# Every second attention head of the last two chunks: scores with tokens on the partitions, one wide transposing DMA, and value products with the values stationary

## The chip, the cores and the metric

The kernel runs on one core of one Trainium2 chip. The metric is the device time of the whole program in microseconds (us). One execution was also recorded by the hardware profiler; the rows of its page and of its trace are what the text argues from. TensorE (PE in the profile) does the matrix products, ScalarE (ACT) the exponentials, VectorE (DVE) copies and elementwise work, GpSimd (POOL) a few tiny operations, and SyncE (SP) issues most DMAs. A "turn" below is a DMA that transposes blocks of 128 x 128 elements on the way.

## The reference

The program is a transformer block with adaptive layer norm on 2048 tokens of width 1024: `x + ga * attention(layernorm(x) * (1 + ca) + sa)`, then the same with a gated feed-forward layer, where the six vectors come from `silu(c) @ w_mod`. The part that the change touches is the attention:

```
q = (x @ wq).reshape(B, Sq, 32, 128)           # 32 query heads of 128
k, v = the last 512 cached keys and values, 4 heads, each repeated for 8 query heads
scores = einsum('bhqd,bhkd->bhqk', q, k) * 128 ** -0.5
p = softmax(scores, axis=-1)
o = einsum('bhqk,bhkd->bhqd', p, v)
return o.transpose(0, 2, 1, 3).reshape(B, Sq, 4096) @ wo
```

## The kernel before

The tokens are worked in 4 chunks of 512. Attention runs in one loop over `i`, where head number `i` goes from 0 to 127 (chunk `i // 32`, head `i % 32`). An iteration of the loop emits, in this order on TensorE: the query projection of head `i + 3` (`qproj`, 8 products 512 columns wide), the scores of head `i - 1` (`scores`, 4 products 512 wide, into the PSUM banks 0 to 3), and the value products of head `i - 2` (`pv`). After the last head of a chunk, `oproj` multiplies the finished heads with `wo` (256 products 512 wide); this place is called the seam. In the last three iterations pieces of the last chunk's `oproj` take the place of `qproj`. The feed-forward layer follows.

In `scores` the keys are stationary, so the exponentials come out with keys on the partitions and tokens along the row: two ACT instructions on 1024 elements a row (L813). `pv` then holds a 128 x 128 block of exponentials stationary and moves the values, with a column of ones beside them, so each product is 129 columns wide and a head takes 16 of them. The 129th column is the sum of the softmax: DVE takes its reciprocal (L831) and multiplies it in (L834), and a turn of 128 x 512 (L837) brings the result from tokens on the partitions to head columns on the partitions, into `oT_all`, which `oproj` reads.

Every operation is emitted through one tracker, which adds semaphore waits for what an operation reads and overwrites. Each engine works through its own instructions in the order of emission, and so does SP's queue of DMAs. An operation of DVE or ACT that overwrites a buffer which the same engine wrote before waits for that engine's own earlier operation.

Other work is spread over the iterations by tables. `LOADT` gives the iterations at which one of 24 columns of `w_mod` is loaded by a turn (`load_mt`, L588); four iterations later `mod_col` multiplies it with `silu(c)` and sums on DVE (L593). `load_wq` (L357) fetches the projection weights of four heads, 1 MB, every fourth iteration. `ln_task` is a generator for the layer norm of a later chunk: statistics, normalisation, a turn of 128 x 1024 (L454), later the scaling; `run_bg(1)` takes one step of it at the end of each iteration. `resid` is the end of an `oproj` product on DVE and uses two tiles `tmp`.

## Time and profile before

| what | us |
|---|---|
| median of 3 runs (lowest, highest) | 1270.17 (1270.08, 1270.31) |
| time of the profiled execution | 1270.14 |
| its span in the profile | 1268.3 |
| TensorE busy | 1255.1 (99%) |
| VectorE busy | 485.1 (38%) |
| ScalarE busy | 341.6 (27%) |

TensorE is busy throughout, at full clock (PEclk 9 in all 40 slices). The other engines' busy shares are means over very different stages: DVE and ACT are busiest in the attention loops, which fill about the first half of the span, and DMA is uneven there. The last two chunks' attention lies between about 362 us, where the second chunk's `oproj` ends, and 640 us; the third chunk's `oproj` stands between them.

### The profile page before, as it was taken

What the parts mean: (1) busy time and instruction counts of PE and PEld (TensorE: products, weight loads), DVE (VectorE), ACT (ScalarE), POOL (GpSimd) and SP (SyncE); (2) the same over time, 40 slices, a digit from 0 to 9 for tenths busy, and PEclk for the clock granted to TensorE, in tenths of its full rate; (3) what the DMA queues carried; (4) which work ended last, traced back from release to release, by engine and by line L of the source; (5) the groups of instructions that cost most, each with busy time, mean ns of one, the idle gap of its engine ahead of it and who ended that gap; (6) DMA issues with size and microseconds to landing.
All of it is one profiled execution on the core that took longest, in us unless ns stands there. A gap on an engine that the chain in (4) does not pass through costs nothing.

```text
span 1268.3 us, 17609 instructions
## 1 busy us (share of the span) xinstructions
PE 1255.1 (99%) x7442; PEld 640.7 (51%) x7583; DVE 485.1 (38%) x894; ACT 341.6 (27%) x389; POOL 56.0 (4%) x95
## 2 busy tenths in 40 slices
PE   8999999999999999999999999999999999999999
PEld 5655545555455554555544444444444444444444
DVE  4676226764257641365322321233212321222122
ACT  4655205553035550155510111011100111011100
POOL 1530000000000000000000000000000000000000
PEclk9999999999999999999999999999999999999999
DMA  9998306875029641064243972055512644034200
GB/s 320 264 263 218 92 1 127 177 171 125 1 57 177 138 114 34 9 129 123 61 145 100 291 246 94 25 158 150 168 40 72 177 141 134 17 128 154 67 9 25
DMA packets 239997, 156.67 MB, mean 124 GB/s; under 512 B 133296, under 2 KB 225840, under 8 KB 239920
## 3 DMA queue, kind: packets, MB, share of 16 engines
q1 hardware_dynamic: 181664, 96.83, 31.6%
q10 hardware_dynamic: 58256, 58.73, 14.6%
q8 instruction: 59, 0.97, 0.3%
q14 instruction: 18, 0.15, 0.1%
HBM read 119.93 MB, written 4.20 MB: 98 GB/s over the span
## 4 chain that ended last, share of the span: by engine, by line
PE 98%; issue 1%; DMA 0%; SPq 0%; DVE 0%
PE ps L271 98%; DMA arena<-in_w_mod_dram 0%; SPq L309 0%; SPq L334 0%; PE ps L275 0%; DVE arena L496 0%; DVE tmp L853 0%; DVE arena L855 0%; DVE gain_f L486 0%
## 5 line engine op out<-in xcount | busy, mean ns | idle before, releaser
L271 PE MATMUL ps<-arena 128*128 128x512 bf16 (+1 forms) x7213 | 1249.3, 333 | 10.1 <-POOL arena L298 2.0
L271 PEld LDWEIGHTS ps<-arena 128*128 128x128 bf16 x7354 | 632.9, 98 | 621.5 <-issue 2.1
L813 ACT ACTIVATE arena<-ps 128x1024 bf16<-128x1024 f32 x256 | 261.9, 1023 | 345.1 <-PE ps L271 333.4
L1059 ACT ACTIVATE arena<-ps 128x512 bf16<-128x512 f32 x112 | 66.9, 597 | 499.6 <-PE ps L271 499.6
L1060 DVE TENSOR_TENSOR arena<-ps,arena 128x512 bf16<-128x512 f32 x112 | 77.5, 692 | 276.2 <-PE ps L271 276.2
L853 DVE TENSOR_TENSOR tmp<-ps,rowb 128x512 f32<-128x512 f32 (+1 forms) x65 | 44.4, 683 | 318.8 <-PE ps L271 318.8
L644 DVE CAST arena<-ps 128x512 bf16<-128x512 f32 x120 | 82.8, 690 | 47.7 <-PE ps L271 47.7
L834 DVE TENSOR_TENSOR arena<-ps,rl 128x512 bf16<-128x512 f32 x128 | 88.5, 691 | 4.7 <-DVE rl L831 0.2
L831 DVE RECIPROCAL rl<-ps 128x4 f32<-128x4 f32 x128 | 23.4, 182 | 114.1 <-PE ps L271 114.1
L429 POOL TENSOR_SCALAR rstd<-mv 128x1 f32<-128x1 f32 x28 | 6.1, 216 | 910.3 <-DVE mv L428 910.3
L424 DVE BATCH_NORM_STATS2 st<-x_res 128x6 f32<-128x512 bf16 x62 | 42.4, 683 | 3.4 <-DMA x_res<-in_A_x_dram 3.3
L593 DVE SCALAR_TENSOR_TENSOR arena<-arena 128x1024 bf16<-128x1024 bf16 x24 | 29.2, 1215 | 0.0
L855 DVE TENSOR_TENSOR arena<-tmp,x_res 128x512 bf16<-128x512 f32 (+2 forms) x33 | 22.3, 677 | 1.1
L855 DVE TENSOR_TENSOR x_res<-tmp,x_res 128x512 bf16<-128x512 f32 x32 | 22.2, 693 | 1.1
L440 DVE TENSOR_SCALAR arena<-arena,gain,mod_bf 128x512 bf16<-128x512 bf16 x56 | 21.2, 420 | 0.0
L435 DVE TENSOR_SCALAR nsc<-x_res,mv,rstd 128x1024 bf16<-128x1024 bf16 x30 | 19.2, 641 | 0.0
L431 POOL TENSOR_TENSOR rstd<-rstd,mhalf 128x1 f32<-128x1 f32 x28 | 15.7, 559 | 2.3
L772 POOL TENSOR_SCALAR arena<-arena,sc_bf 128x512 f32<-128x512 bf16 x8 | 12.9, 1614 | 0.5 <-POOL arena L774 0.2
L774 POOL TENSOR_TENSOR arena<-arena 128x512 f32<-128x512 f32 x8 | 10.1, 1265 | 0.7
L428 DVE BATCH_NORM_AGGREGATE mv<-st 128x2 f32<-128x12 f32 x28 | 5.8, 209 | 1.0
L271 PEld LDWEIGHTS ps<-sc_bf,arena 128*128 128x128 bf16 x128 | 4.4, 96 | 1.4 <-DMA arena<-in_w_mod_dram 0.3
L271 PE MATMUL ps<-sc_bf,arena 128*128 128x1 bf16 x128 | 4.7, 164 | 0.3 <-DMA arena<-in_w_mod_dram 0.3
(56 smaller groups left out, 59.4 us busy)
## 6 DMA issues: line engine op xcount, KB each, us to landing
arena<-in_A_wq_dram SPq DMA_DIRECT2D x30, 1024.0 KB, 5.8
arena<-in_B_w_gate_dram ACTq DMA_DIRECT2D x28, 1024.0 KB, 5.4
arena<-in_B_w_up_dram ACTq DMA_DIRECT2D x28, 1024.0 KB, 7.9
arena<-in_A_wo_dram SPq DMA_DIRECT2D x8, 1024.0 KB, 7.6
arena<-in_B_w_down_dram SPq DMA_DIRECT2D x7, 1024.0 KB, 8.3
out_dram<-arena SPq DMA_DIRECT2D x15, 256.0 KB, 2.0
x_res<-in_A_x_dram SPq DMA_DIRECT2D x3, 1024.0 KB, 7.0
arena<-arena SPq DMA_TRANSPOSE x132, 2.6
```

What stands on the lines that cost most here:

```text
L271: T.op(PE, lambda: TE.matmul(out_ap, lhsT, rhs, start=start, stop=stop, skip_group_check=skip), reads=reads, writes=[bank_buf])
L424: T.op(DVE, lambda: V.bn_stats(st_[sl][:, hf * 6:hf * 6 + 6], x_res[:, t, hf * 512:hf * 512 + 512]), reads=[B_x[t]], writes=[B_st[sl]])
L440: T.op(DVE, lambda: V.tensor_scalar(dst[:, dt, :], dst[:, dt, :], gain[gi][:, dt:dt + 1], mod_bf[:, ccol + dt:ccol + dt + 1], op0=ALU.mult ...
L593: T.op(DVE, lambda: V.scalar_tensor_tensor(mt[n % 2], mt[n % 2], 1.0, sc_row, op0=ALU.mult, op1=ALU.mult, accum_out=mcol[:, n:n + 1]), rea ...
L644: T.op(DVE, lambda: V.tensor_copy(qT_s[qs], bank(b)), writes=[PB[b], B_qT[qs]])
L813: T.op(ACT, lambda: A.activation(ex_s[es][:, 2 * kp:2 * kp + 2, :], banks2(SCB + 2 * kp), AF.Exp, scale=att_scale), writes=[PB[SCB + 2 * k ...
L831: T.op(DVE, lambda: V.reciprocal(rl[r][:, :].rearrange("p (a b) -> p a b", a=2), psap(PVB * 512 + P, [[512, 2], [130, 2]])), writes=both + ...
L834: T.op(DVE, lambda: V.tensor_tensor(o_s[os_].rearrange("p (a b) d -> p a b d", a=2), psap(PVB * 512, [[512, 2], [130, 2], [1, P]]), rlb, A ...
L853: T.op(DVE, lambda: V.tensor_tensor(tmp[s][:, 0:n], bank(b, n), rowb[ri][:, c0:c0 + n], ALU.mult), reads=[B_row[ri]], writes=[PB[b], B_tmp ...
L855: T.op(DVE, lambda: V.tensor_tensor(dst[:, c0:c0 + n], tmp[s][:, 0:n], x_res[:, t, c0:c0 + n], ALU.add), reads=[B_tmp[s], B_x[t]], writes= ...
L1059: T.op(ACT, lambda: A.activation(sg_s[ss], bank(gb), AF.Silu), writes=[PB[gb], B_sg[ss]])
L1060: T.op(DVE, lambda: V.tensor_tensor(guT[:, ft, :], bank(ub), sg_s[ss], ALU.mult), reads=[B_sg[ss]], writes=[PB[ub], B_gu[ft]])
```

## The change

Heads 66, 68, ..., 126 (31 heads, the set `NAT`) go another way. Heads 64 and all odd heads keep theirs.

- `nat_scores`: the queries of 128 tokens are stationary and all 512 keys move, 4 products 512 wide. The exponentials have tokens on the partitions; they are four ACT instructions on 512 elements a row, and each also gives the sum of its row (`accum_out`). They are emitted one iteration earlier than `scores` would be, in the odd iteration before, in the place that the missing `scores` leaves.
- `nat_norm`: DVE takes the reciprocals of the sums and multiplies them in, in two halves: a reciprocal of 128 x 2 and two in-place `tensor_scalar` of 128 x 512 each, from bf16 to bf16 in SBUF. The first half follows `pv` in the odd iteration, the second follows `qproj` in the even one.
- `nat_turn`: one turn of 128 x 2048 (512 KB) brings keys onto the partitions.
- `nat_pv`: the values are stationary, the turned exponentials move: 4 products 512 wide into one bank. The result already stands in the layout of `oT_all`, and one DVE copy out of PSUM puts it there. The turn of 128 x 512 (L837), the reciprocal of 128 x 4 and the multiplication of 128 x 512 are gone for these heads. `nat_pv` comes two iterations after the head's turn is issued.
- At a seam (iterations 65 and 97) `nat_scores` and both halves of `nat_norm` come after `pv` and before `oproj`, and the turn after `oproj`.
- The buffers: the exponentials of these heads alternate between the first of the two `ex` tiles and the two `tmp` tiles, which become one tensor. The turned ones lie in two slots of 4 KB whose place moves twice (`PTAT`).
- `load_wq` is emitted before the scores, not behind `pv`, from iteration 65 on. The loads of `w_mod` columns go to every second iteration (33, 35, ..., 79) where they were 9 iterations to 4; what follows the last of them comes 6 iterations earlier. `run_bg` is called in other iterations, twice in some.

The diff, cut to its core:

```diff
+            NAT0 = 2 * Hq + 2
+            NAT = set(range(NAT0, NA, 2))
+            B_pn = [[_Buf("pn0_%d" % hf) for hf in range(2)], B_tmp]
+            pn = [None, tmp_t[:, :].bitcast(BF16)]
...
+            def nat_scores(i):
...
+                for j in range(TPC):
+                    mm(bank(SCB + j), qT_s[qs][:, j * P:(j + 1) * P],
+                       kT_sb[:, gk * KT:(gk + 1) * KT, :].rearrange("p a b -> p (a b)"), True, True,
+                       [B_kT[gk], B_qT[qs]], PB[SCB + j])
+                for j in range(TPC):
+                    T.op(ACT, lambda: A.activation(pn[s][:, j * 512:(j + 1) * 512], bank(SCB + j), AF.Exp, scale=att_scale,
+                                                   accum_out=psum[s][:, j:j + 1]),
+                         writes=[PB[SCB + j], B_pn[s][j // 2], B_psum[s][j // 2]])
+
+            def nat_norm(i, hf):
+                s = p_slot(i)
+                T.op(DVE, lambda: V.reciprocal(pinv[s][:, 2 * hf:2 * hf + 2], psum[s][:, 2 * hf:2 * hf + 2]),
+                     reads=[B_psum[s][hf]], writes=[B_pinv[s][hf]])
+                for j in (2 * hf, 2 * hf + 1):
+                    pj = pn[s][:, j * 512:(j + 1) * 512]
+                    T.op(DVE, lambda: V.tensor_scalar(pj, pj, pinv[s][:, j:j + 1], None, op0=ALU.mult),
+                         reads=[B_pinv[s][hf]], writes=[B_pn[s][hf]])
+
+            def nat_turn(i):
+                s = p_slot(i)
+                pt_of[i] = (pt[s], B_pt[s])
+                T.op(Q_pt[s], lambda: SP.dma_start_transpose(pt[s], pn[s]), reads=B_pn[s], writes=[B_pt[s]])
+
+            def nat_pv(i):
...
+                for kt in range(KT):
+                    mm(bank(PVB).rearrange("p (j q) -> p j q", j=TPC), v_aug[:, gk * KT + kt, 0:P], ptv[:, :, kt, :],
+                       kt == 0, kt == KT - 1, [B_va, B_vg[gk], pb], PB[PVB])
+                T.op(DVE, lambda: V.tensor_copy(oT_all[:, h, :], bank(PVB)), writes=[PB[PVB], B_oT[h]])
...
-            LOADT = {Hq + 2 + (9 * n) // 4: n for n in range(NL)}
+            LOADT = {Hq + 1 + 2 * n: n for n in range(NL)}
...
+            PTAT = {2 * Hq + 2: OFF_OT + 24 * KB, 2 * Hq + 24: OFF_H20, 3 * Hq: OFF_HT}
...
+                if i % 4 == 1 and i >= NAT0 - 1:
+                    load_wq((i + 4) // 4 + 1)
...
+                seam = (i - 1) % Hq == 0 and i + 1 in NAT
+                if i + 1 in PTAT and not seam:
+                    pt_region(PTAT[i + 1])
+                if i in NAT and (i - 2) % Hq:
+                    nat_norm(i, 1)
+                    nat_turn(i)
+                nat = i % 2 == 1 and i + 1 in NAT
+                if nat and not seam:
+                    if i - 4 not in LOADT:
+                        run_bg(1)
+                    nat_scores(i + 1)
-                if 1 <= i - 1 < NA:
+                if 1 <= i - 1 < NA and i - 1 not in NAT:
                     scores(i - 1)
                 if 0 <= i - 2 < NA:
-                    pv(i - 2)
+                    if i - 2 in NAT:
+                        nat_pv(i - 2)
+                    else:
+                        pv(i - 2)
+                    if nat:
+                        if seam:
+                            nat_scores(i + 1)
+                        nat_norm(i + 1, 0)
+                        if seam:
+                            nat_norm(i + 1, 1)
...
                     if h2 == Hq - 1 and ch2 < NCH - 1:
                         oproj(ch2)
-                run_bg(1)
+                        if seam:
+                            if i + 1 in PTAT:
+                                pt_region(PTAT[i + 1])
+                            nat_turn(i + 1)
+                if not nat or seam:
+                    run_bg(2 if i in NAT and i % 4 == 2 and i - 3 in LOADT else 1)
```

More of the change, by code (lines that the diff above doesn't have):

```diff
@@ L197, in bass_adaLN_cond__sliding_block_cached__swiglu_ffn__prompt_kernel @@
     rl = [S_("rl%d" % i, [P, 4], F32) for i in range(2)]
+    psum = [S_("psum%d" % i, [P, 4], F32) for i in range(2)]
+    pinv = [S_("pinv%d" % i, [P, 4], F32) for i in range(2)]
     nsc = [S_("nsc%d" % i, [P, D], BF16) for i in range(2)]
-    tmp = [S_("tmp%d" % i, [P, 512], F32) for i in range(2)]
+    tmp_t = S_("tmp", [P, 1024], F32)
+    tmp = [tmp_t[:, i * 512:(i + 1) * 512] for i in range(2)]
     KB = 1024
@@ L245, in bass_adaLN_cond__sliding_block_cached__swiglu_ffn__prompt_kernel @@
     B_rl = [_Buf("rl%d" % i) for i in range(2)]
+    B_psum = [[_Buf("psum%d_%d" % (i, hf)) for hf in range(2)] for i in range(2)]
+    B_pinv = [[_Buf("pinv%d_%d" % (i, hf)) for hf in range(2)] for i in range(2)]
     B_ns = [_Buf("ns%d" % i) for i in range(2)]
@@ L839, in pv, with p_slot, pt_region @@
                      reads=[B_os[os_]], writes=[B_oT[h]])
+            NAT0 = 2 * Hq + 2
+            NAT = set(range(NAT0, NA, 2))
+            B_pn = [[_Buf("pn0_%d" % hf) for hf in range(2)], B_tmp]
+            pn = [None, tmp_t[:, :].bitcast(BF16)]
+            B_pt = [_Buf("pt%d" % s) for s in range(2)]
+            pt = [None, None]
+            pt_of = {}
+            Q_pt = [dq("q_pt%d" % i) for i in range(2)]
+            def p_slot(i):
+                return (i - NAT0) // 2 % 2
+            def pt_region(off):
+                for s in range(2):
+                    B_pt[s] = _Buf("pt%d" % s)
+                    pt[s] = arena.at(off + s * 4 * KB, [TPC * KT, P], BF16, [B_pt[s]])
@@ new lines, in nat_scores @@
+            def nat_scores(i):
+                gk = i % Hq // rep
+                qs = q_slot(i)
+                s = p_slot(i)
+                if pn[0] is None:
+                    pn[0] = arena.at(OFF_EX, [TPC * KT * P], BF16, B_pn[0])
+                for j in range(TPC):
[6 more added lines that the diff above has]
+                         writes=[PB[SCB + j], B_pn[s][j // 2], B_psum[s][j // 2]])
@@ new lines, in nat_turn @@
+            def nat_turn(i):
+                s = p_slot(i)
+                pt_of[i] = (pt[s], B_pt[s])
+                T.op(Q_pt[s], lambda: SP.dma_start_transpose(pt[s], pn[s]), reads=B_pn[s], writes=[B_pt[s]])
+            def nat_pv(i):
+                h = i % Hq
+                gk = h // rep
+                s = p_slot(i)
+                pa, pb = pt_of.pop(i)
+                ptv = pa.rearrange("p (j k) q -> p j k q", j=TPC)
+                for kt in range(KT):
+                    mm(bank(PVB).rearrange("p (j q) -> p j q", j=TPC), v_aug[:, gk * KT + kt, 0:P], ptv[:, :, kt, :],
+                       kt == 0, kt == KT - 1, [B_va, B_vg[gk], pb], PB[PVB])
+                T.op(DVE, lambda: V.tensor_copy(oT_all[:, h, :], bank(PVB)), writes=[PB[PVB], B_oT[h]])
@@ L895, in _ @@
             GATES = {26: 0, 27: 1}
-            t2 = Hq + 6 + (9 * (NL - 1)) // 4
+            t2 = Hq + 5 + 2 * (NL - 1)
             TURNT = (28, t2 + 1)
-            PUTT = {33: (0, c_sil, B_csil), 30: (1, mrow[0:DT, :], B_mrow), t2 + 3: (2, mrow[0:DT, :], B_mrow)}
+            PUTT = {33: (0, c_sil, B_csil), 30: (1, mrow[0:DT, :], B_mrow), t2 + 2: (2, mrow[0:DT, :], B_mrow)}
             GETT = {35: (0, sc_row, B_scr), 31: (1, rowb[0][:, :], B_row[0]), t2 + 4: (2, rowb[1][:, :], B_row[1])}
-            LOADT = {Hq + 2 + (9 * n) // 4: n for n in range(NL)}
+            LOADT = {Hq + 1 + 2 * n: n for n in range(NL)}
             LOADO = {5 + (21 * p) // 8: p for p in range(8)}
             LOADK = {1: 1, 5: 2, 6: 3}
+            PTAT = {2 * Hq + 2: OFF_OT + 24 * KB, 2 * Hq + 24: OFF_H20, 3 * Hq: OFF_HT}
             for i in range(1, NA + 2):
@@ L958, in _ @@
                     oproj_mm(NCH - 1, 1, XB, 8 * (n - 3), 8 * (n - 3) + 8)
-                if 1 <= i - 1 < NA:
+                seam = (i - 1) % Hq == 0 and i + 1 in NAT
[10 more added lines that the diff above has]
+                if 1 <= i - 1 < NA and i - 1 not in NAT:
                     scores(i - 1)
                 if 0 <= i - 2 < NA:
-                    pv(i - 2)
+                    if i - 2 in NAT:
[8 more added lines that the diff above has]
+                            nat_norm(i + 1, 1)
                     ch2, h2 = divmod(i - 2, Hq)
-                    if i % 4 == 1 and i > 5:
+                    if i % 4 == 1 and 5 < i < NAT0 - 1:
                         load_wq((i + 4) // 4 + 1)
```

## The prediction

> **What bounds the kernel now.** First the page's busy shares and its chain that ended last.

> ```profile
> span 1268.3 us, 17609 instructions
> PE 1255.1 (99%) x7442; PEld 640.7 (51%) x7583; DVE 485.1 (38%) x894; ACT 341.6 (27%) x389; POOL 56.0 (4%) x95
> ...
> PE 98%; issue 1%; DMA 0%; SPq 0%; DVE 0%
> ```

> TensorE is the bound and hardly waits; the list of waits names no wait of PE inside the attention. So the change can gain only what it takes off TensorE's own stream, and loses what it makes TensorE wait. The stage comes next: a timeline of two iterations, then the groups by shape.

> ```profile
> 620.28 0.69 DVE L644 CAST arena<-ps 128x512 bf16<-128x512 f32 x1 [0.82 <-PE ps L271]
> 620.71 2.14 ACT L813 ACTIVATE arena<-ps 128x1024 bf16<-128x1024 f32 x2 [1.36 <-PE ps L271]
> 622.05 0.18 DVE L831 RECIPROCAL rl<-ps 128x4 f32<-128x4 f32 x1 [1.08 <-PE ps L271]
> 622.27 0.69 DVE L834 TENSOR_TENSOR arena<-ps,rl 128x512 bf16<-128x512 f32 x1
> 624.21 2.14 ACT L813 ACTIVATE arena<-ps 128x1024 bf16<-128x1024 f32 x2 [1.36 <-PE ps L271]
> 625.55 0.18 DVE L831 RECIPROCAL rl<-ps 128x4 f32<-128x4 f32 x1 [2.59 <-PE ps L271]
> ```

> An iteration is 3.50 us (622.05 to 625.55), paced by PE: ACT and DVE wait for it. The starts of single products in the trace are 0.2158 us apart for 512 columns and 0.0566 for 129; 12 and 16 of them make 2.590 + 0.906 = 3.496 us, so there is no hole.

> ```profile
> L675 DVE TENSOR_SCALAR arena<-arena,mod_bf 128x512 bf16<-128x512 bf16 x8 | 2.2, 348 | 0.0
> ...
> L1059 ACT ACTIVATE arena<-ps 128x512 bf16<-128x512 f32 x112 | 66.9, 597 | 499.6 <-PE ps L271 499.6
> ...
> L518 ACT ACTIVATION_READ_ACCUMULATOR arena<-x_res 128x1 f32 x1 | 0.2, 187 | 0.0
> ```

> These are the nearest rows for the new DVE and ACT work. Last the turns: in a quiet stretch (540 to 541 us) one 512 and one 1024 wide, then their issue times on SP.

> ```profile
> arena<-arena SPq DMA_TRANSPOSE x1, 2.4
> arena<-nsc SPq DMA_TRANSPOSE x1, 3.1
> ...
> L837 SPq DMA_TRANSPOSE arena<-arena x128: 1188/1192/2657, 35.0 to 639.6; - x128
> L454 SPq DMA_TRANSPOSE arena<-nsc x28: 1232/1250/2732, 57.0 to 1018.1; - x28
> ```

> Doubling the width adds 0.65 us to the landing (2.41 to 3.06 in the trace) and 0.06 us to the issue.

> **TensorE's part.** Per head of the 31: 4 score products 512 wide before and after; 16 x 0.0566 = 0.906 us of value products become 4 x 0.2158 = 0.863. Gain 0.043 x 31 = 1.3 us. The moving operand now steps in runs of 128; no row shows that on PE. Bounds: no cost, or one product start more per run (0.0566 - 129/512 x 0.2158 = 0.002 us), 16 x 0.002 = 0.03 us a head, 1.0 us in all; I take none, since contiguous rows of both widths fit one rate.

> [...]

> **First seam.** In iteration 65 the scores of head 66 follow `pv` by 0.9 us behind those of head 64. Their third bank is free when head 64's second exponential ends: it starts 0.63 + 1.12 us after the scores of 64, takes 1.02, so 2.8 us; the third product is due after 0.86 + 0.91 + 0.43 = 2.2 us. Cost 0.6 us, once; at the second seam `scores` is missing before it.

> **ACT.** Each exponential: 0.597, the read of the sum overlaps by 0.09 and takes 0.187, and 0.06 to 0.09 for the wait on the engine's own last write: about 0.75 us a step, 3.0 against 2.14. The scores of the odd iteration start at 1.73 us in it (time zero is the start of `qproj`), exponentials at 2.14, end 5.1. The last bank is wanted at 3.50 + 1.73 + 0.65 = 5.87. Hidden, 0.7 us to spare.

> **DVE.** A half: reciprocal 0.2, two `tensor_scalar` of 0.35 that wait for each other, 0.37 a step: 0.95. A pair of iterations: two casts 1.22 (0.61 a step), reciprocal and multiplication of the odd head 0.81, two halves 1.9, the copy 0.61: 4.5 us of 6.95; before 2.84. With `mod_col` (1.26, until iteration 83) and one and a half layer norm steps (1.0) 6.8: full, still no queue that grows. The tightest consumer, the next `qproj` into its one bank, has its cast done at 2.9 of 3.5 us. Hidden.

> **The turn.** It decides. Multiplication of the odd head ends at 4.6; first half 5.5; cast 6.1; second half 7.05; issue 7.05 (7.3 with a late weight's DMA ahead on SP). A turn of 2048: 2.41 + 3 x 0.65 = 4.4 us, landing at 11.4 to 11.7. `nat_pv` starts at 6.95 + 3.50 + 1.73 + 0.86 = 13.0. Slack 1.3 to 1.6 us. Bounds of the turn alone: below, the backlog rate (516 packets of 256 B in 0.5 us at 565 us): 1.17 + 2.0 + 0.4 = 3.6; above, 4 x 2.41 = 9.6. I take 4.4, from the two widths in rows.

> Queued behind the waiting `nat_turn` on SP are layer norm turns and `load_wq`; the weights are used 13.9 us after issue and land 5.4 to 7.5 us after it, so they stand the delay. But DMAs land nearly in order: at 546.06 a 512 turn behind a weight load took 6.4 us. With the old turn of the pair before, a layer norm turn and 1 MB ahead (iterations 69, 73, 77, 81), the queue works: old turn to 3.9, layer norm 4.9, weights 7.6 to 8.5, odd head's turn 9.0, late weight 10.0, new turn 12.0, landed 11.5 to 12.4. Slack 0.5 to 1.4. In the other pairs 1.2 to 1.6.

> Instruction fetches break in: one 16 KB fetch per 15.6 us in the trace (562.8, 578.2, 594.1, 608.6); where it meets a turn, that lands about 1.5 us late (the turn at 622.99: 3.9 instead of 2.41). Four tight pairs, hit six times in ten (10 us of queue against 15.6), late by 0.5 us: 1.2 us. The other 27: 2.3 us of turn, four hits, 0.2 us each: 0.8. Stalls 2.0 us.

> [...] The backlog row above is 264 GB/s.

> **At nothing.** The earlier `load_wq` only gains time for landing. The late weights are the same 24 turns and DVE steps, with DVE idle as cover. Two 512 turns per pair on SP become one and a wide one (1.19 + 1.37 us of 6.95). The copy out of PSUM ends 1.5 us before `pv` wants the bank. The row of late weights (a turn, a 2 KB store and its load, moved 6 iterations ahead) is read by the feed-forward alone; the third place of the turned tiles waits for nothing younger than two iterations. The layer norm of the last chunk takes 19 steps, three per four iterations up to 83 and one each then, so it ends near 89, before 93 wants it. The new exponentials' tile was last read by the turn of four iterations before, landed 2 us ahead. The last head has 0.86 us less slack, as iteration 127 has no scores, but no weights in its queue. If DVE's cover goes, the turn is late: below.

> **Sum.** -1.3 + 0.6 + 2.0 = +1.3, on 1270.14 of the profiled execution (span 1268.3 and 1.84 around it; the median 1270.17 is the same within 0.03): 1271.4, I say 1271.2, since hits can overlap. 0.2% (2.5 us) is about what a measurement can tell from no change.

> **Rivals.**

> A. As above, with stalls from none (-0.7: 1269.5) to 3.2 us (+2.5: 1272.7). Chance 0.50. The sign within it is open; its own range is 1269.0 to 1272.7.

> B. The turn is late by tenths in nearly every pair: a wider turn is dearer than two widths tell, or the queue is. Two turns are in flight, and the scores of the next head come ahead of the stalled `nat_pv`, so a lateness x beyond the slack costs x per two pairs: 15.5 x. Slower by 0.2% from x = 0.21 us; at 0.5 us -0.7 + 7.8 = +7.1, 1277.2. For it: DMA share 1.01 from 376 to 384 us already. Against: 0.19 from 605 to 640. Chance 0.29.

> C. Landing grows with width, 9.6 us: x = 9.6 - 4.4 - 1.4 = 3.8, +59, 1328. For it, the highest landings in the trace (8.1 us); against, 2.41 to 3.06. Chance 0.07.

> D. DVE becomes the bound: if its in-place `tensor_scalar` took 0.69 as PSUM operands do, 1.4 us more per pair. The nine pairs with `mod_col` would run at 8.2 instead of 6.95: +11, and the turn would be 0.2 late elsewhere, +2: 1283. Against, 348 ns on just this shape. Chance 0.09.

> E. The other side: weight loads pace the short products. The page's loads take 98 ns each; if 16 of them took 1.57 us where 4 wide products take 0.86, 0.7 x 31 = 22 us would go, 1248. It decides once a load is not covered by the product ahead; the measured 56.6 ns speaks against. With any gain unseen here, 0.05. [...]

> Chances: faster 0.05 (E), within 0.2% 0.50 (A), slower 0.45 (B, C, D). The range leaves out E, C and most of D and takes in B to x = 0.8: 1268.9 to 1282.

> **What would show it.** Starts of value products 0.216 us apart, four a head; turns of 2048 landing 4.4 us after issue when alone; PE waiting for `arena<-arena` DMAs only in chunk 2 up to iteration 81 and at fetches, and for ACT once at the first seam; DVE's copies with idle time ahead of them. I am wrong if those waits come in nearly every pair, if the wide turn lands after 6 us alone, or if a wait on DVE's cast appears.

## The result, and the profile after

| what | us |
|---|---|
| before, median of 6 runs (lowest, highest) | 1270.24 (1270.08, 1272.41) |
| after, median of 6 runs (lowest, highest) | 1276.82 (1274.80, 1277.48) |
| ratio after to before, 95% interval | 1.0049 (1.0038 to 1.0059) |
| profiled execution, before and after | 1270.14 and 1276.27 |

The changed kernel is slower by 0.5%. The predicted range (1268.9 to 1282) held the time; the forecast of no measurable change did not. The profiled execution is 6.13 us longer than that of before, and those 6.13 us are what the following lines account for.

First the page of after: span, busy times, and the chain that ended last.

```profile
span 1274.5 us, 17290 instructions
PE 1256.8 (99%) x7076; PEld 625.0 (49%) x7211; DVE 527.8 (41%) x1049; ACT 360.4 (28%) x575; POOL 55.9 (4%) x95
PE 95%; DMA 3%; DVE 1%; issue 1%; ACT 0%
```

TensorE is still the bound. DMA, which held 0% of the chain before, now holds 3%. Next the list of waits for 362 to 640 us, the attention of the last two chunks. The columns are the wait, its total in us, how often, the longest. In this stretch of the kernel before PE had no such lines.

```profile
PEld ps L276 <- DMA arena<-arena: 6.0, 4, 2.9
PE ps L276 <- DMA arena<-arena: 4.0, 4, 2.4
PE ps L276 <- DMA arena<-tmp: 0.4, 1, 0.4
```

L276 is the line of every product, and `arena<-arena` and `arena<-tmp` are here the wide turns: `nat_pv` waits for exponentials that are not turned yet. There is no PE line that names DVE. Outside this stretch there is one more new wait, in the timeline of PE at the first seam:

```profile
306.08 2.12 PE L276 MATMUL ps<-arena 128*128 128x512 bf16 x9 [0.46 <-ACT arena L818]
```

The third score product of head 66 waited for head 64's exponentials to free its bank. From start to start of the products that is 0.63 us lost; the row's idle time leaves out about 0.16 us of every such hole.

Measured in this way, from start to start, the stalls at the wide turns are these. "Landing" counts from the turn's issue; 14 of the 31 wide turns, none with a fetch inside, took 4.24 to 4.38 us, and 4.5 is the median of all.

| head | stall at (us) | stall (us) | turn's landing after its issue (us) | instruction fetch inside the landing |
|---|---|---|---|---|
| 70 | 388.08 | 2.59 | 5.83 | 384.38 |
| 76 | 411.16 | 0.53 | 5.87 | 407.27 |
| 78 | 418.70 | 0.58 | 4.44 (issued late) | none |
| 82 | 433.66 | 1.05 | 7.05 | 431.31 |
| 110 | 586.70 | 0.47 | 6.17 | 584.46 |
| 116 | 607.64 | 0.08 | 5.92 | 605.28 |

They sum to 5.30 us. The other 25 heads do not stall. One more hole is too short for the list of waits: 0.24 us at 372.46, where the first product of a `qproj` follows the query cast (L649), which ends at 372.32. The largest stall, head 70's, has a second price, in the timeline of PE and in two windows (length; busy time of PE, PEld, DVE, ACT and POOL; then the granted clock, the DMA share and GB/s):

```profile
388.08 1.72 PE L276 MATMUL ps<-arena 128*128 128x512 bf16 x4 [2.42 <-DMA arena<-arena]
390.02 2.30 PE L276 MATMUL ps<-arena 128*128 128x512 bf16 x6 [0.22 <-issue]
```

```profile
384.88:388.29 3.41, 0.99 (x5) 0.28 (x4) 1.73 (x5) 2.05 (x2) 0.00 (x0) 1.00 0.73 155
388.29:391.70 3.41, 3.19 (x8) 1.22 (x8) 1.15 (x2) 0.00 (x0) 0.00 (x0) 0.50 0.91 182
```

After 2.42 us of idle time the clock granted to TensorE is 0.50 for 3.41 us: four products take 1.72 us, where at full clock they take 0.86. Eight products start 0.427 us apart instead of 0.216, and 8 x 0.211 = 1.69 us are lost on top of the stall. Five of the six executions show a granted clock of 0.999 over the whole; the sixth shows 1.000 and is the fastest, at 1274.80 us.

The account: value products -31 x 0.043 = -1.33 (the query casts, one per iteration, come 0.04 us earlier per pair in stretches without stalls); seam +0.63; the hole at the cast +0.24; stalls +5.30; half clock +1.69. The sum is +6.53. From the first residual step on DVE to the last, the two profiled executions differ by 6.57. Behind the last one the execution of before takes 2.83 us and that of after 2.39, which brings the difference of the whole down to the measured 6.13.

Why head 70's turn was late shows in SP's timeline (start, duration of the issue). Its data were ready on DVE at 379.43 us, but it was issued at 382.21.

```profile
372.13 1.30 SPq L593 DMA_TRANSPOSE arena<-in_w_mod_dram  x1
373.47 2.16 SPq L890 DMA_TRANSPOSE arena<-tmp  x1
375.68 1.66 SPq L459 DMA_TRANSPOSE arena<-nsc  x1
377.44 0.53 SPq L362 DMA_DIRECT2D arena<-in_A_wq_dram  x1
378.01 1.32 SPq L842 DMA_TRANSPOSE arena<-arena  x1
379.37 2.73 SPq L593 DMA_TRANSPOSE arena<-in_w_mod_dram  x1
382.21 3.80 SPq L890 DMA_TRANSPOSE arena<-arena  x1
```

L593 is a late column, L890 the wide turn, L459 the layer norm's turn, L362 the 1 MB of weights, L842 the narrow turn of the odd head. The column's issue took 1.30 us at 372.13, with one narrow turn still in flight, and 2.73 at 379.37, with the weights and a narrow turn in flight. The wide turn's own issue took 3.80 with these two and the column in flight, and 1.53 at 635.69, with one narrow turn. So SP's issues took longer here where more DMAs were still in flight.

One word on what is computed: at the first seam the exponentials of head 66 are written at 306 to 309 us into the tile that holds those of head 64, and `pv` of head 64 reads it only after `oproj`, at about 365 us. So head 64 of the third chunk is not what the reference asks for. The instructions and their times are the same. The kernels below that derive from the changed one share this, but for the two that move head 64's `pv` ahead.

### The profile page after: what moved, and what is told of

Read it like the earlier page. It is cut to its first block, busy times and chain, and to the rows that moved or that the text cites. A ratio compares the mean times of both kernels' runs of the same rounds, so it can differ in the third digit from the quotient of the medians.

```text
span 1274.5 us, 17290 instructions
## 1 busy us (share of the span) xinstructions
PE 1256.8 (99%) x7076; PEld 625.0 (49%) x7211; DVE 527.8 (41%) x1049; ACT 360.4 (28%) x575; POOL 55.9 (4%) x95
## 4 chain that ended last, share of the span: by engine, by line
PE 95%; DMA 3%; DVE 1%; issue 1%; ACT 0%
PE ps L276 95%; DMA arena<-arena 2%; DVE st L429 1%; DMA arena<-tmp 0%; DMA x_res<-in_A_x_dram 0%; PE ps L280 0%; DVE arena L649 0%; DVE arena L901 0%; DVE arena L839 0%; DVE arena L598 0%; ACT arena L818 0%; DVE nsc L440 0%; DVE tmp L884 0%; DVE mv L529 0%; DVE mv L433 0%
## 5 line engine op out<-in xcount | busy, mean ns | idle before, releaser
L276 PE MATMUL ps<-arena 128*128 128x512 bf16 (+1 forms) x6847 | 1251.1, 342 | 14.8 <-DMA arena<-arena 4.0
L276 PEld LDWEIGHTS ps<-arena 128*128 128x128 bf16 x6982 | 617.3, 98 | 643.7 <-DMA arena<-arena 6.0
L818 ACT ACTIVATE arena<-ps 128x1024 bf16<-128x1024 f32 x194 | 198.7, 1024 | 286.3 <-PE ps L276 277.4
L1149 ACT ACTIVATE arena<-ps 128x512 bf16<-128x512 f32 x112 | 66.9, 597 | 500.2 <-PE ps L276 500.2
L649 DVE CAST arena<-ps 128x512 bf16<-128x512 f32 x120 | 82.6, 688 | 40.3 <-PE ps L276 40.3
L839 DVE TENSOR_TENSOR arena<-ps,rl 128x512 bf16<-128x512 f32 x97 | 67.1, 691 | 3.6 <-DVE rl L836 0.2
L836 DVE RECIPROCAL rl<-ps 128x4 f32<-128x4 f32 x97 | 17.7, 182 | 68.8 <-PE ps L276 68.7
L874 ACT ACTIVATE arena<-ps 128x512 bf16<-128x512 f32 x64 | 37.9, 595 | 27.0 <-PE ps L276 22.0
L874 ACT ACTIVATE tmp<-ps 128x512 bf16<-128x512 f32 x60 | 35.6, 595 | 19.9 <-PE ps L276 17.1
L598 DVE SCALAR_TENSOR_TENSOR arena<-arena 128x1024 bf16<-128x1024 bf16 x24 | 29.1, 1215 | 0.0
L901 DVE CAST arena<-ps 128x512 bf16<-128x512 f32 x31 | 21.4, 691 | 14.4 <-PE ps L276 14.3
L884 DVE TENSOR_SCALAR arena<-arena,pinv 128x512 bf16<-128x512 bf16 x64 | 22.6, 353 | 2.3
L884 DVE TENSOR_SCALAR tmp<-tmp,pinv 128x512 bf16<-128x512 bf16 x60 | 21.2, 353 | 2.1
```

The costliest lines, as they stand in the source:

```text
L276: T.op(PE, lambda: TE.matmul(out_ap, lhsT, rhs, start=start, stop=stop, skip_group_check=skip), reads=reads, writes=[bank_buf])
L598: T.op(DVE, lambda: V.scalar_tensor_tensor(mt[n % 2], mt[n % 2], 1.0, sc_row, op0=ALU.mult, op1=ALU.mult, accum_out=mcol[:, n:n + 1]), rea ...
L649: T.op(DVE, lambda: V.tensor_copy(qT_s[qs], bank(b)), writes=[PB[b], B_qT[qs]])
L818: T.op(ACT, lambda: A.activation(ex_s[es][:, 2 * kp:2 * kp + 2, :], banks2(SCB + 2 * kp), AF.Exp, scale=att_scale), writes=[PB[SCB + 2 * k ...
L839: T.op(DVE, lambda: V.tensor_tensor(o_s[os_].rearrange("p (a b) d -> p a b d", a=2), psap(PVB * 512, [[512, 2], [130, 2], [1, P]]), rlb, A ...
L874: T.op(ACT, lambda: A.activation(pn[s][:, j * 512:(j + 1) * 512], bank(SCB + j), AF.Exp, scale=att_scale, accum_out=psum[s][:, j:j + 1]), ...
```

## The experiments

Theory 1: the wide turns are late through the amount of data in the DMA queue ahead of them, in pairs of iterations that also carry a layer norm turn, a column and 1 MB of weights; an instruction fetch in the middle adds to it. Theory 2: the data are a smaller matter, and it is the late column whose issue blocks SP just ahead of the wide turn. A third reading has nothing to do with DMA: the DVE and ACT work, or the strided operand of the value products. A fourth is named in some expectations: the instruction fetches alone.

**No turn.** The turn is left out for all heads but six, so the products of the others multiply old data; all else stays.

```diff
-                T.op(Q_pt[s], lambda: SP.dma_start_transpose(pt[s], pn[s]), reads=B_pn[s], writes=[B_pt[s]])
+                if i in (66, 68, 88, 90, 96, 98):
+                    T.op(Q_pt[s], lambda: SP.dma_start_transpose(pt[s], pn[s]), reads=B_pn[s], writes=[B_pt[s]])
```

> Leaves out 25 of the 31 wide turns (each slot of the turned tiles is filled once per place and then read again), so most value products read old exponentials; every other instruction stays. Theory 1 (the loss is the late turns and the half clock behind the longest of them): TensorE gains 1.3 us and loses 0.6 us at the first seam, 1269.5 us, ratio 0.9994, no wait of TensorE inside the last two chunks but the one at the seam. Rival (DVE or ACT hold TensorE up, or the strided moving operand is slower than 0.216 us a product): the time stays near the changed kernel's, 1275 us or more.

Measured: 1269.69 us, ratio 0.9993 (0.9984 to 1.0003). The list of waits for 300 to 640 us names one wait of PE, and the window in which the changed kernel lost most is full:

```profile
PE ps L276 <- ACT arena L818: 0.5, 1, 0.5
```

```profile
362.00:400.00 38.00, 37.92 (x248) 20.01 (x246) 34.06 (x80) 23.98 (x51) 2.33 (x6) 1.00 0.67 143
```

What is left is the seam and the 0.24 us behind the query cast (at 372.78 here). DVE is busy for 34 of 38 us and PE hardly waits for it: the third reading falls. The value products with the strided operand start 0.2158 us apart, as contiguous ones do. The loss belongs to the wide turns, their transfers and the waits for them.

**Columns earlier.** A column comes every 4/3 iterations instead of every second one, so that nearly all lie ahead of the wide turns, and its DVE step follows 2 iterations behind instead of 4. The calls of `run_bg` keep the old table.

```diff
-            LOADT = {Hq + 1 + 2 * n: n for n in range(NL)}
+            LOADT = {Hq + 3 + (4 * n) // 3: n for n in range(NL)}
-                if i - 4 in LOADT:
-                    n = LOADT[i - 4]
+                if i - 2 in LOADT:
+                    n = LOADT[i - 2]
```

> The loads of the 24 late weight columns go to iterations 35 to 65, four iterations to three loads, their DVE step two iterations behind; all else as in the changed kernel. Theory 1 (what counts is the work in the DMA queue ahead of the turn in the pairs that also load weights): 1 us less ahead of the turns of heads 70 to 80, the first stall falls from 2.4 us to 1 us or less, no half clock, sum of stalls 1.5 to 2.5 us: 1271 to 1272, ratio 1.001. Theory 2 (SP sits in the issue of the late weight, which blocks the issue of the turn): the same or better, 1270 to 1271. Rival (the stalls come from instruction fetches alone): two or three stalls stay and the time is 1274 or more.

Measured: 1300.18 us, 1.0235 (1.022 to 1.025). A miss, by a new wait in the second chunk. Its list of waits from 200 to 320 us:

```profile
DVE arena L598 <- DMA arena<-in_w_mod_dram: 30.2, 12, 5.2
PE ps L276 <- DVE arena L839: 16.8, 7, 3.7
```

Two iterations are too short: DVE stood in `mod_col` (L598) for a column queued behind weights, and PE stood behind DVE's multiplication (L839), with four half-clock stretches. In the last two chunks the stalls at wide turns were down to 1.33, 0.72 and 0.64 us, which fits theory 1, but the run says little alone.

**Columns in even iterations.** The column's issue is moved out of the place just ahead of the wide turn. Its DVE step then comes in even iterations too; `run_bg` keeps the old table.

```diff
-            LOADT = {Hq + 1 + 2 * n: n for n in range(NL)}
+            LOADT = {Hq + 2 + 2 * n: n for n in range(NL)}
```

> The late weight columns are loaded in the even iterations, behind the wide turn on SP, not in the odd ones ahead of it; the same number of DMAs in the same stretch. Theory 1 (the amount in the queue): the column goes from ahead of this turn to ahead of the next, in the tight pairs the same amount stands ahead of the turn, so 1274 to 1277, ratio 1.004. Theory 2 (the issue on SP is blocked): the turn of head 70 is issued at once when DVE is done, 2.8 us earlier, the long stall and the half clock go: 1270.5 to 1272.

Measured: 1283.38 us, 1.0099 (1.0082 to 1.0117): slower than both theories gave. Waits of PE, 362 to 640 us:

```profile
PE ps L276 <- DMA arena<-arena: 8.4, 4, 3.6
```

Head 70's turn was now issued 0.9 us earlier (381.31), but this issue took 4.41 us and the turn landed 8.02 us after it, at 389.33 instead of 388.04. It stalled PE for 3.37 us and head 82 for 3.74, each with half clock behind it (3.41 and 6.83 us long). An earlier place in SP's order buys nothing where the data ahead are the same: theory 2 by itself falls. One part is confounded, since `mod_col` (1.2 us) now also lies ahead of the second half of `nat_norm` on DVE.

**Layer norm step in the other pair.** The double step of the layer norm, and with it the turn of 128 x 1024, goes to the iterations without weights.

```diff
-                    run_bg(2 if i in NAT and i % 4 == 2 and i - 3 in LOADT else 1)
+                    if i != NAT0:
+                        run_bg(2 if i in NAT and i % 4 == 0 and i - 3 in LOADT else 1)
```

> The layer norm steps of the last chunk shift by two iterations, so that its turns fall into the pairs without a weight load. Theory 1 (the amount in the queue): 1 us less ahead of the turns of heads 70, 74, 78, 82; the long stall falls to 1.4 us, the half clock goes, the other pairs' slack of more than 1 us takes the layer norm: 1271.5 to 1273, ratio 1.0015. Theory 2 (SP's issue blocked by the late weight): the column's issue stays behind a weight load, the stall stays over 2 us: 1275 or more.

Measured: 1274.46 us, 1.0032 (1.0022 to 1.0042): above theory 1's 1271.5 to 1273 and below theory 2's 1275, a miss of both. Waits of PE, 362 to 640 us:

```profile
PE ps L276 <- DMA arena<-arena: 1.8, 4, 0.9
PE ps L276 <- DMA arena<-tmp: 1.7, 1, 1.7
```

Head 70's stall fell from 2.59 to 1.07 us, and its half clock is gone. But head 76, whose pair now holds the layer norm turn, a column and a fetch (405.9), rose from 0.53 to 1.86; 74, 82 and 110 lost 0.37, 0.57 and 0.42. Theory 1 had counted on the slack of these pairs to hide the layer norm turn, and it did not. The stall goes where the DMAs go.

**No weights.** `load_wq` is left out from iteration 65 on, so the later heads are projected with old weights.

```diff
-                if i % 4 == 1 and i >= NAT0 - 1:
-                    load_wq((i + 4) // 4 + 1)
```

> Leaves out the loads of query weights from iteration 65 on, so the heads behind them are projected with older weights; all else as in the changed kernel. Theory 1 (work in the DMA queue ahead of the turn, most of all the 1 MB): every pair is like the pairs without weights, the turns land 4.3 to 4.6 us after issue but for an instruction fetch, no stall over 0.7 us, no half clock: 1269.5 to 1271, ratio 1.000. Rival (the late weight and the layer norm alone make the turns late, or the fetches do): the stalls of heads 76 or 82 stay over 0.7 us and the time is 1273 or more.

Measured: 1271.2 us, 1.0007 (0.9998 to 1.0016). Waits of PE, 362 to 640 us:

```profile
PE ps L276 <- DMA arena<-arena: 0.9, 1, 0.9
```

Without the 1 MB loads 5.6 of the 6.6 us between the two medians are gone. Head 70 still loses 1.07 us, where at most 0.7 was expected: a column, the layer norm turn and a fetch at 384.3 are enough for that. Heads 76 and 68 lose 0.40 and 0.14.

**How long a hole halves the clock.** This is the kernel before, with holes of growing, then of shrinking length in the products of `oproj`: the first product of each group waits for k copies on DVE.

```diff
+                    if ch in (1, 2) and k > 0:
+                        pb_ = [QB, XB][(k - 1) % 2]
+                        for _ in range(k if ch == 1 else 8 - k):
+                            T.op(DVE, lambda: V.tensor_copy(nsc[0][:, 0:512], bank(pb_)), writes=[PB[pb_], B_ns[0]])
+                        oproj_mm(ch, k, b, 0, 1, [B_ns[0]])
+                        oproj_end(ch, k - 1, pb_)
+                        oproj_mm(ch, k, b, 1, Hq)
+                        if k == 2 * TPC - 1:
+                            oproj_end(ch, k, b)
+                        continue
```

> The kernel before, with holes cut into TensorE's stream in the output projections of the second and third chunk: ahead of seven products each, the first matmul waits for 1 to 7 copies of 0.6 us on VectorE; nothing is left out. Holes of about 1.0, 1.6, 2.2, 2.8, 3.4, 4.0 and 4.6 us, rising and then falling. If a stall halves the clock by its length alone, every hole from some length between 1.7 and 2.4 us on is followed by products 0.427 us apart for about 3.4 us, in both orders, and none below; the loss per hole is then its length and 1.7 us. Rival (the half clock behind head 70's stall came from something else, such as the state of the whole stretch): holes of 2.2 to 2.8 us leave the products at 0.216 us.

Measured: 1329.48 us in one run; what counts are the single holes. The timeline of PE has two with the same idle time (in brackets); then come, for each of them, the window of 3.41 us that holds most of its idle time and the window behind it. Why these windows is said below.

```profile
341.60 7.08 PE L271 MATMUL ps<-arena 128*128 128x512 bf16 x31 [2.96 <-DVE nsc L876]
552.64 8.53 PE L271 MATMUL ps<-arena 128*128 128x512 bf16 x31 [2.96 <-DVE nsc L876]
```

```profile
337.16:340.57 3.41, 1.48 (x7) 0.49 (x5) 1.83 (x3) 0.00 (x0) 0.00 (x0) 1.00 0.01 2
340.57:343.98 3.41, 2.38 (x11) 1.09 (x12) 2.32 (x4) 0.00 (x0) 0.00 (x0) 1.00 0.02 5
548.79:552.20 3.41, 0.89 (x5) 0.20 (x2) 2.38 (x4) 0.00 (x0) 0.00 (x0) 1.00 0.00 0
552.20:555.61 3.41, 2.97 (x8) 1.05 (x9) 1.76 (x3) 0.00 (x0) 0.00 (x0) 0.50 0.02 5
```

| hole, start to start (us) | 0.95 | 1.67 | 2.40 | 3.12 | 3.85 | 4.58 | 5.30 |
|---|---|---|---|---|---|---|---|
| growing | full | full | full | full | half | half | half |
| shrinking | full | full | full | half | half | half | half |

A threshold between 1.7 and 2.4 us, the same in both orders, was expected; this missed. The hole of 3.12 us left the clock alone at 341.60 and halved it at 552.64 (7 products at the half rate). Taken over all runs, ten holes of 1.7 to 2.40 us never halved it, and of 16 from 2.59 us up 14 did, one of 4.07 us (below) not. So length alone does not decide between about 2.4 and 4.1 us.

What else decides can be read from the granted clock. Inside the kernels of all runs a half-clock stretch is 3.41 or 6.83 us long, and the stretches of one run start whole multiples of 3.41 us apart (here at 350.81, 364.47 and 378.12, for instance). These lengths and starts fit a clock that is set in windows of 3.41 us which take no notice of the holes. Cut into these windows, the traces that have a half-clock stretch to place them by show the half clock behind each of the 14 full-clock windows in which PE was busy for 0.05 to 0.41 of the time, and behind none in which it was busy for 0.43 or more. The first hole of 3.12 us is split between two windows and leaves 1.48 of 3.41 us busy (0.43); the other lies almost wholly in one and leaves 0.89 (0.26). Head 70's hole of 2.59 us leaves 0.99 (0.29). So the place of a hole within its window decided here, not its length alone. Behind the holes that halved it the products ran at the half rate for 3.0 to 5.8 us, which cost 1.5 to 2.9.

**Layer norms and last columns in the seams.** The layer norm of the last chunk and that of the feed-forward's first chunk run during `oproj`, three steps after each of its products, and so do the last eight loads of columns and nine of their DVE steps, in the first seam. The same DMAs are issued in all; none of these is left beside wide turns.

```diff
-                if h == 2 and 1 <= ch < NCH - 1:
-                    add_ln1(ch + 1)
-                if h == 2 and ch == NCH - 1:
-                    add_ln2(0)
+                if h == 2 and ch == 1:
+                    add_ln1(2)
+                if i == 2 * Hq + 1:
+                    add_ln1(3)
+                if i == 3 * Hq + 1:
+                    add_ln2(0)
...
-                run_bg(1)
+                run_bg(3 if ch in (1, 2) else 1)
...
+                    if ch == 1:
+                        col_done(15 + k)
+                        load_mt(16 + k) if k == 0 else None
+                        load_mt(17 + k) if k < 7 else None
...
-            LOADT = {Hq + 1 + 2 * n: n for n in range(NL)}
+            LOADT = {Hq + 1 + 2 * n: n for n in range(16)}
```

(`col_done` is `mod_col` with what follows the last column of a group.)

> The layer norm of the last chunk and that of the feed-forward's first chunk move into the two seams, where VectorE and the DMA queue are idle, and so do the last 8 late weight columns and 9 of their steps on VectorE; the alternate heads are as in the changed kernel. Theory 1: only turns and query weights are left in the queue, stalls of 0.3 to 1.0 us in all, no half clock: -1.3 + 0.6 + 0.3 to 1.0, 1269.8 to 1270.5, ratio 0.9997 to 1.0003. Rival (the query weights alone make the turns late): 1272 or more.

Measured: 1269.78 us, 0.9996 (0.9987 to 1.0005), as expected. Two stalls are left, 0.16 and 0.12 us, and the seam's 0.63. Every wide turn is still there, with the 1 MB of weights in every second pair. That is theory 1, and it shows that the loss is no property of the wide turn. The landing times of the wide turns (L890) also settle the fourth reading:

```profile
DMA to landing us min/median/max: 4.2/4.3/6.2
```

The turns of heads 76, 82, 110 and 116 still land 5.96 to 6.16 us after their issue, with a fetch inside, and at most 0.16 us of stall comes of it. In this run a fetch alone did not make a turn too late; in the changed kernel it did where the queue had used up the slack (0.47 to 2.59 us for heads 70, 76, 82 and 110).

**The seam's order too.** In addition head 64's `pv`, head 66's scores and `nat_norm` are emitted behind the first product of `oproj`, so that ACT has its time.

```diff
+                    if ch == 1 and k == 0:
+                        pv(2 * Hq, False)
+                        nat_scores(2 * Hq + 2)
+                        nat_norm(2 * Hq + 2, 0)
+                        nat_norm(2 * Hq + 2, 1)
```

> The same, and at the first seam the value products of head 64 and the scores of head 66 come behind the first product of the output projection. That takes away the 0.6 us wait for the score banks, and the exponentials of head 66 no longer overwrite those of head 64 before they are read. Theory 1: 1269.2 to 1269.9, ratio 0.9992 to 0.9998, faster than both kernels. Rival: as for the run before, less 0.6 us.

Measured: 1269.63 us, 0.9995 (0.9987 to 1.0004): in the expected range, but with an interval that reaches no change. The wait for ACT is gone, but a new one came at the seam's end (timeline of PE):

```profile
367.17 2.99 PE L276 MATMUL ps<-arena 128*128 128x512 bf16 x16 [0.67 <-DVE arena L649]
```

L649 is the query cast; on DVE a residual step and one step of `mod_col` (1.22 us) lay ahead of it, and the second step of `mod_col` stood behind it. The hole took 0.83 us, more than the seam's 0.63 that it replaced.

**The last two column steps later.** They move from the seam's end to iterations 69 and 71.

```diff
-                    if ch == 1:
+                    if ch == 1 and k < 7:
...
-                if i == 2 * Hq + 2:
-                    col_done(NL - 1)
+                if i in (2 * Hq + 5, 2 * Hq + 7):
+                    col_done(NL - 2 + (i - 2 * Hq - 5) // 2)
```

> As the run before with the seam's new order, but the last two steps of the late weight columns wait for iterations 69 and 71, so that VectorE has nothing but the residual ahead of the first query cast behind the seam. If the 0.7 us wait of TensorE at that place came from these two steps (1.2 us each ahead of the cast), it goes and nothing takes its place: 1269.0 us against 1269.6, ratio 0.9990. Rival (the wait has another cause): no change.

Measured: 1269.05 us, against 1270.38 for the kernel before on the same chip: 0.9991 (0.9982 to 1.0). The window of 362 to 400 us:

```profile
362.00:400.00 38.00, 38.00 (x236) 19.60 (x235) 25.98 (x62) 24.55 (x52) 0.00 (x0) 1.00 0.68 146
```

PE is busy throughout at full clock, and the DMA share is 0.68. This is the changed kernel's own gain laid bare: the products give -1.33 us, two gaps of 0.09 and 0.07 take 0.16 back, and from the first residual step on DVE to the last the profiled executions differ by -1.15. It is ahead of both kernels by median, though the interval reaches no change.

**Columns three iterations behind.** After the second experiment's wait, a milder form of it; again `run_bg` keeps the old table.

```diff
-            LOADT = {Hq + 1 + 2 * n: n for n in range(NL)}
+            LOADT = {Hq + 3 + (3 * n) // 2: n for n in range(NL)}
-                if i - 4 in LOADT:
-                    n = LOADT[i - 4]
+                if i - 3 in LOADT:
+                    n = LOADT[i - 3]
```

> The late weight columns early once more, in iterations 35 to 69, three iterations to two loads, but with three iterations between a load and its VectorE step where the first try had two; all else as in the changed kernel. If the waits of the first try came from VectorE standing in that step until a column that was queued behind query weights had landed, they go from the second chunk, and theory 1 is left with stalls of 1.5 to 3 us in the last two chunks and no half clock: 1271 to 1273, ratio 1.0015. If they stay, the steps themselves are too much for VectorE: 1280 or more.

Measured: 1277.57 us, 1.0055 (1.0041 to 1.0068). A miss. The waits for DVE in the second chunk are gone, as expected, but PE waits from 362 to 640 us for

```profile
PE ps L276 <- DMA arena<-arena: 5.0, 3, 3.9
```

The last three columns fell into iterations 66, 68 and 69, and two of them (issued at 375.59 and 381.10 us) into the queue ahead of head 70's turn, which cost 4.07 us; heads 82 and 110 lost 0.66 and 0.74. This hole did not halve the clock, and the trace has no half-clock stretch from which its windows could be told. The profiled execution took 1275.05 us, 2.5 us below the median. The other three show a granted clock of 0.997 to 0.999 where this one shows 1.000, so they had half clock in addition; behind which hole is not seen.

**The same without its last three columns.** They are not loaded, so that the feed-forward's modulation uses old numbers there.

```diff
-                    if i in LOADT:
+                    if LOADT.get(i, NL) < 21:
                         load_mt(LOADT[i])
```

> As the second try with early late weight columns, but the loads of the last three columns, which fell into iterations 66, 68 and 69 and so into the tightest pair, are left out (their three steps run on the old tile). Theory 1: the 4.1 us stall of head 70 falls to 1.5 us or less, since only the layer norm and the query weights stand ahead of its turn; heads 82 and 110 keep stalls of 0.5 to 0.8 us at instruction fetches: 1271 to 1272.5, ratio 1.001. If the stall of head 70 stays over 3 us, the columns are not its cause.

Measured: 1272.57 us, 1.0019 (1.0009 to 1.0028).

Head 70's stall went from 4.07 to 1.78 us, somewhat over the expected 1.5. Its turn's issue now began on time (379.61), but took 4.19 us, and the turn landed 7.67 us after its start, with a fetch inside: nothing ahead of it on SP made it late, the queue did.

**Only the layer norms into the seams.** The first two edits of "layer norms and last columns in the seams", without the columns.

```diff
+                if i == 2 * Hq + 1:
+                    add_ln1(3)
+                if i == 3 * Hq + 1:
+                    add_ln2(0)
...
-                run_bg(1)
+                run_bg(3 if ch in (1, 2) else 1)
```

> Of the changes in the two seams only the layer norms: the late weight columns stay in iterations 33 to 79 as in the changed kernel. Theory 1 (each microsecond ahead of the turn in a pair with query weights counts): the pairs have the columns and query weights, but no layer norm; stalls of 1 to 2.5 us in all, no half clock: 1270.5 to 1272.5, ratio 1.001. If the columns are the cause by themselves, 1274 or more; if the layer norm is, 1270 or less.

Measured: 1271.02 us, 1.0005 (0.9996 to 1.0015), as expected, with

```profile
PE ps L276 <- DMA arena<-arena: 1.7, 2, 0.9
PE ps L276 <- DMA arena<-tmp: 0.7, 1, 0.7
```

Stalls of 1.11, 0.85 and 0.89 us (heads 70, 76, 78), and no half clock. With the columns gone too, 0.28 us of stalls remained. The shares do not add up to the loss: without the layer norms alone 5.8 of the 6.6 us are gone, without the weights alone 5.6. Each brings the queue ahead of the turn nearly within the slack, and only what is beyond the slack costs.

Head 70's stall over these runs, with what was taken from or added to the queue ahead of it. In all of them an instruction fetch falls into the landing of its turn.

| queue ahead of head 70's turn | stall (us) |
|---|---|
| column, layer norm turn, weights (changed kernel) | 2.59 |
| the same, the column in an even iteration | 3.37 |
| two columns, layer norm turn, weights | 4.07 |
| layer norm turn, weights (two runs) | 1.78, 1.33 |
| column, weights (layer norm in the seam, or in the other pairs) | 1.11, 1.07 |
| column, layer norm turn; no weights | 1.07 |
| weights alone, in the seam runs (at most 0.16 over all heads) | 0 |

Each transfer taken away shortens it, whichever it is. That is theory 1. SP's blocked issue goes with it: the issues are long in the rows where the DMAs are behind (3.80 us for the changed kernel's wide turn, 2.06 with weights alone). That the one follows from the other is a reading that no run tests by itself.

## Why the prediction was right or wrong

**TensorE's part: right.** The gain is 0.04 us per head, and the strided operand is free. The upper bound of 1.0 us for it can be dropped. Rival E falls: with 25 turns gone nothing hid a gain of 22 us, and the spacing stays 0.2158 us for 512 columns.

**First seam: right.** 0.6 predicted, 0.63 measured.

**ACT and DVE: right, but for one wait.** The groups of after, 362 to 640 us (busy us and mean ns, then idle time ahead of them):

```profile
L874 ACT ACTIVATE tmp<-ps 128x512 bf16<-128x512 f32 x60 | 35.6, 595 | 19.9 <-PE ps L276 17.1
L874 ACT ACTIVATION_READ_ACCUMULATOR tmp<-ps 128x1 f32 x60 | 11.8, 196 | 0.0
L884 DVE TENSOR_SCALAR tmp<-tmp,pinv 128x512 bf16<-128x512 bf16 x60 | 21.2, 353 | 2.1
```

0.595, 0.196 and 0.353 us stand against 0.597, 0.187 and 0.35 in the working. The four steps of a head on ACT take 2.83 us, with starts 0.78 and 0.59 us apart in turn, against 3.0; a half on DVE takes 0.94 against 0.95. Rival D had no case. A wait on DVE's cast, named as a sign of being wrong, did appear, once and with 0.24 us.

**The turn alone: right.** 4.4 us was taken between bounds of 3.6 and 9.6, and the turns of heads 120, 124 and 126, issued with one narrow turn in flight, landed after 4.25 to 4.26. Rival C falls. 512 KB in 4.3 us, issue and landing included, are 122 GB/s. The shortest issue is 1.53 us, 1.37 was assumed. The turns out of the `ex` tile, min, median and max of the issue in ns:

```profile
L890 SPq DMA_TRANSPOSE arena<-arena x16: 1527/3018/3796, 362.0 to 635.7; - x16
DMA to landing us min/median/max: 4.2/4.5/7.0
```

The median issue of these 16 is 3.02 us, twice the shortest: the case "alone" is not the usual one for SP.

**The turn in the queue: the step that failed.** The stalls were summed to 2.0 us ("Four tight pairs, hit six times in ten, late by 0.5 us: 1.2 us. The other 27: four hits, 0.2 us each: 0.8"). Measured: 5.3 us in six stalls. The number of stalls was about right, and five of the six have a fetch inside, the mechanism that the working named. What was mis-sized is the tight pairs: heads 70, 78 and 82 lost 4.22 us where 1.2 was summed; the other three stalls come to 1.08 against 0.8. The walk through the queue of such a pair shows where. Times are us from the start of iteration 69 (372.45); the walk says when the queue is through with a transfer, the trace when it has landed.

| transfer | walk | landed |
|---|---|---|
| wide turn of head 68 | 3.9 | 5.5 |
| layer norm turn | 4.9 | 6.8 |
| weights, 1 MB | 7.6 to 8.5 | 11.2 |
| turn of the odd head | 9.0 | 11.7 |
| column | 10.0 | 14.0 |
| wide turn of head 70 (landing in both) | 11.5 to 12.4 | 15.6 |
| value products due | 13.0 | 13.0 |

The queue was late from the first row on, and the weights and the column took still longer than the walk gave them; between 385 and 386 us, behind the fetch at 384.38, the DMAs moved 6 GB/s, where they had moved 171 to 252 in the two us before. SP shows the same: the working issued the wide turn at 7.05 to 7.3. In fact the column's issue took 2.73 us with the weights still in flight, and the wide turn's 3.80, so that head 70's turn went out at 9.8, 2.8 us after its data were ready. The slack in such a pair was put at 0.5 to 1.4 us; head 70 was 2.59 us beyond it.

**What was not in the sum: the half clock.** A stall had been priced at its own length. The one of 2.59 us cost another 1.69 through the clock. Over the six, 5.3 + 1.7 = 7.0 us stand where the sum had 2.0; with this the sum of the prediction would be 1276.4, near the 1276.27 of the profiled execution and the median of 1276.82.

**The rivals.** A was the forecast and fell, on the size of its stalls and the half clock behind the longest; its own range ended at 1272.7. That the whole range held the time is luck: it reached so far for the sake of B. B gave 1277.2 us, near the time, but by another mechanism: "late by tenths in nearly every pair" would be fifteen waits, one for every two pairs, also from 440 to 640 us, where only two small ones stand. What is measured has A's places, with a size in the tight pairs that neither had. Of the signs named beforehand, "PE waiting for `arena<-arena` DMAs only in chunk 2 up to iteration 81 and at fetches" came true, and that sign was for A.

**The half clock: one hole stays open.** The hole of 4.07 us that did not halve the clock stays open, since its trace does not show where its windows lie; had they split it near the middle, each would have kept a share of about 0.43 (an estimate from its 3.91 us of idle time and the 3.41).

## What to carry to other kernels

A transfer that is given a deadline is to be priced with the queue that it meets at its tightest place, and the issues ahead of it with what they take while that queue is busy (here 1.53 became 3.80 us), not by its own landing in a quiet stretch. Where one place of the schedule is tight, move the other DMAs out of it before judging the idea: the same change was 0.5% slower with layer norm turns and columns beside it, and within 0.1% of the kernel before with them in the seams. And do not price a TensorE stall at its own length alone. A hole that left PE busy for up to 0.41 of one 3.41 us window halved the clock here and cost 1.5 to 2.9 us more; by that share a hole of 2.0 us could do it (an estimate, 0.59 x 3.41), and the shortest that did was 2.59.
